# An attention-then-MLP kernel on one core: its opening re-ordered, with ungated loads, weight loads tied to landings, and mask products and casts moved between engines

## The chip, the core and the metric

The kernel runs on one core of a Trainium2 chip. The core has TensorE (PE in the profile; its weight loads are PEld), VectorE (DVE), ScalarE (ACT), GpSimd (POOL) and SyncE (SP), each with an instruction queue of its own that it works through in order, and 16 DMA engines that all queues share. The metric is the time of one execution in device microseconds (us), median of 3 runs.

## The reference

Attention with a decay per head, in blocks over the sequence, followed by a two-layer MLP with a leaky slope per hidden unit. Inputs and output are fp32; B, H, S, D = 4, 8, 768, 64; the MLP has 512 inputs and outputs and 2048 hidden units.

```python
rel = pos[:, None] - pos[None, :]
Dmask = np.where(rel >= 0, lam[:, None, None] ** rel, 0.0)
for b in range(S // block):
    qb, kb, vb = q[:, :, sl], k[:, :, sl], v[:, :, sl]      # sl: block b
    intra = (qb @ kb.T * Dmask) @ vb                         # per batch and head
    inter = (qb * lam ** (pos + 1)) @ kv_state
    out[:, :, sl] = intra + inter
    kv_state = lam ** block * kv_state + (kb * lam ** (block - 1 - pos)).T @ vb
x = out.transpose(0, 2, 1, 3).reshape(B * S, H * D)
h = x @ w_in
y = (np.maximum(h, 0) + alpha * np.minimum(h, 0)) @ w_out
```

## The kernel before, in words

**Tiling.** The 3072 tokens are cut into 6 chunks `c` of 512 tokens. A chunk is 256 positions (two blocks of 128) of two batches `bi`, and each batch is cut into two halves of four heads, `hh`. Such a quarter of a chunk is a *unit*: units 0 to 3 are chunk 0, 4 to 7 chunk 1, and so on to 23. `load(c, bi)` (line 81) loads k, q and v of one batch of a chunk, three DMAs of 512 KB issued from SP (the first, for chunk 0, in two halves of 256 KB); so `load(0, 0)` feeds units 0 and 1, `load(0, 1)` units 2 and 3. There are five raw buffers of each of k, q and v. `load_win(i)` and `load_wout(i)` (lines 95, 101) load a quarter of each weight from the POOL queue, 512 KB once they are fp16; quarter `i` of w_in serves hidden tiles `f` = 4i to 4i+3.

**A unit's attention.** `casts(n, eng)` (line 209) turns k, q, v into fp16 on the three engines that the three letters of `eng` name (V is DVE, A is ACT, G is POOL), and makes `kdec`, k times its decay, on POOL. `transposes(n)` (line 229) turns k and q on PE and copies the result to `qkT` on DVE; `decayed(n)` (line 246) makes `qdT`, q times its decay, on POOL. `cluster(old, new)` (line 260) issues on PE the products with the state (`qdT` by `RD`) and `sm` by v of unit `old`, and the scores `s` and the state update of unit `new`; DVE multiplies `s` by `dmask` into `sm` and updates the state `R`, POOL copies `R` to `RD` for the next cluster, and ACT copies the finished output of `old` to `xT`. `decay_mask(hp)` (line 167) makes the masks of a pair of heads: an exponential on ACT and a product with `keep` on POOL for each head.

**The MLP.** `up(c, f, bi)` (line 370) is four PE products for hidden tile `f` of chunk `c`, then ACT `m` (L388) and DVE `g` (L397); without `bi` it takes the whole chunk (512 columns, a *full* up), with it one batch (256 columns, a *half* up). Early ups rotate over three PSUM buffers. `down(c, t, part, 4)` (line 404) is four products of the second layer; after the fourth part ACT evacuates and issues the store.

**Order.** The order within each engine is that of the program text (`manual_schedule`), and it is written out by hand for chunks 0 and 1 (lines 466 to 541). From line 543 a rule takes over: `weave` spreads the ten attention steps of the next chunk evenly between ups of this chunk and downs of the last. The first such weave lies between lines 543 and 544 and has 16 downs of chunk 0 and units 8 to 11. Two small DMAs, `gate(0, ...)` and `gate(1, ...)` (lines 501, 536), read from w_in's third and w_out's third quarter and stand in SP's queue ahead of the loads of chunk 1 and of chunks 2 and 3, so that those are issued only when the weight quarters have landed. The transfers issued from SP and ACT (hardware_dynamic in the profile: the loads and the stores) take turns on eight DMA semaphores, and an issue waits until the transfer that had its semaphore has landed.

Of the kernel before, what the change touches and what calls it, by code (L numbers as in the profile page):

```python
# [11 lines left out]
def kernel(  # L12
# [195 lines left out]

    def casts(n, eng):
        c, bi, hh = units[n]  # L210
        kr, qr, vr = (
            t[:, ds(4 * hh, 4), :].rearrange("p h (e d) -> p e h d", e=2) for t in raws[c, bi]
        )
        t = T[n] = {}
        for name, src, e in zip(("k16", "q16", "v16"), (kr, qr, vr), eng):
            t[name] = half_pool.tile([128, 2, 4, D], fp16, tag=name, name=name)
            copy_on(e, t[name], src)
        if True:
            kdec = half_pool.tile([128, 2, 4, D], fp16, tag="kdec", name="kdec")
            for e in range(2):  # L220
                nc.gpsimd.tensor_tensor(  # L221
                    out=kdec[:, e],
                    in0=kr[:, e],
                    in1=kdecay[:, ds(4 * hh, 4), e].unsqueeze(2).to_broadcast([128, 4, D]),
                    op=ALU.mult,
                )
            t["kdec"] = kdec
# [290 lines left out]
    load_wout(1)  # L518
    for f in range(6):
        up(1, f, 0, True)  # L520
    transposes(6, "V")
    for f in range(6, 8):
        up(1, f, 0, True)
    cluster(None, 6)
# [63 lines left out]
```

## Time and profile before

| | us |
|---|---|
| median of 3 runs | 256.09 (255.88 to 256.97) |
| profiled execution | 256.11 |
| its span, first to last instruction | 254.0 |
| PE busy in the span | 215.7 (85%) |
| DVE, ACT, POOL busy | 139.3, 110.3, 116.8 |

The profiled execution is the median to within 0.02 us, and 2.1 us of it lie outside the span. PE is the busiest engine. Where a row has "[1.62 <-POOL RD L364]", the engine stood idle for 1.62 us before that instruction and the thing named ended the wait. A busy PE is not PE at its peak, since the ends of matmuls are modelled; the length of a run of equal matmuls tells its pace.

### The profile page before, as it was taken

Reading aid. Unit: us, or ns where it says so; the run is one execution under the profiler, and the core shown is the slowest. Engines: PE = TensorE matmul, PEld = TensorE weight load, DVE = VectorE, ACT = ScalarE, POOL = GpSimd, SP = SyncE. Lnnn points to the kernel's source line nnn. Section 1 sums busy time; section 2 is a strip of 40 time slices with the busy share of each in tenths; the row PEclk is TensorE's granted clock in tenths of the full one; section 3 lists DMA queues with packets and bytes.
Section 4 is the critical chain, followed back from the end, with each engine's and each line's share of the span. In section 5 each row is a group of like instructions: output and inputs, shape, how many; then the busy total and the mean of one; then the engine's idle time right before and its main releaser. Section 6 shows DMA issues by size and latency. Waiting matters only on the chain.

```text
span 254.0 us, 5553 instructions
## 1 busy us (share of the span) xinstructions
PE 215.7 (85%) x2233; PEld 119.8 (47%) x2233; DVE 139.3 (55%) x284; ACT 110.3 (43%) x210; POOL 116.8 (46%) x225
## 2 busy tenths in 40 slices
PE   0445669749687989699999999999999999999994
PEld 0323556337463554245555455554555544444453
DVE  6414767756976545147676476763676653443100
ACT  4912346525376121244544544446345453444211
POOL 3899536177604688643476437647274600000000
PEclk9999999977999999799999999999999999999999
DMA  5994997016899999999101110111011101111122
GB/s 145 291 161 69 177 305 183 3 6 105 119 228 291 290 310 301 296 320 266 45 3 43 44 41 3 41 44 41 3 41 44 41 5 41 41 41 44 41 83 83
DMA packets 45517, 29.72 MB, mean 117 GB/s; under 512 B 1316, under 2 KB 42548, under 8 KB 45492
## 3 DMA queue, kind: packets, MB, share of 16 engines
q1 hardware_dynamic: 37524, 18.89, 28.6%
q0 software_dynamic: 4224, 4.19, 11.2%
q10 hardware_dynamic: 3744, 6.30, 6.7%
q8 instruction: 17, 0.28, 0.5%
q14 instruction: 8, 0.07, 0.1%
HBM read 27.28 MB, written 6.29 MB: 132 GB/s over the span
## 4 chain that ended last, share of the span: by engine, by line
PE 68%; POOL 9%; DMA 8%; DVE 6%; ACT 4%; issue 3%; ACTq 0%; POOLq 0%; DVEq 0%
PE h_ps L380 30%; PE o_ps L410 24%; PE o_ps L433 5%; DMA kraw<-in_k_dram 3%; DMA qraw<-in_q_dram 3%; DVE g L397 2%; PE tp L235 2%; POOL qdT L250 2%; POOL dmask L171 2%; PE acc L304 2%; ACT m L388 2%; PE s L292 2%; PE acc L275 2%; DMA lam_sb<-in_lam_dram 2%; POOL RD L364 1%
## 5 line engine op out<-in xcount | busy, mean ns | idle before, releaser
L397 DVE SCALAR_TENSOR_TENSOR g<-m,oma,h_ps 128x512 f16<-128x512 f32 (+1 forms) x118 | 75.2, 647 | 73.4 <-ACT m L388 72.5
L380 PE MATMUL h_ps<-xT,w_in_sb 128*128 128x512 f16 (+1 forms) x472 | 102.1, 353 | 3.0 <-DVE g L397 1.1
L388 ACT ACTIVATE m<-h_ps 128x512 f32<-128x512 f32 (+1 forms) x118 | 61.1, 517 | 71.9 <-PE h_ps L380 69.3
L410 PE MATMUL o_ps<-w_out_sb,g 128*128 128x512 f16 x320 | 82.3, 382 | 2.6 <-DVE g L397 1.5
L380 PEld LDWEIGHTS <-w_in_sb 128*128 128x128 f16 x472 | 46.6, 102 | 41.4 <-issue 6.7
L410 PEld LDWEIGHTS <-g 128*128 128x128 f16 x320 | 30.0, 98 | 36.6 <-issue 4.4
L250 POOL TENSOR_TENSOR qdT<-qkT,qdecay 128x512 f16<-128x512 f16 x24 | 27.9, 1162 | 42.0 <-DVE qkT L205 41.7
L330 DVE TENSOR_TENSOR sm<-s,dmask 128x512 f16<-128x512 f32 x48 | 31.0, 684 | 12.3 <-POOL dmask L171 6.6
L364 POOL COPY RD<-R 64x128 f16<-64x128 f16 x80 | 23.6, 294 | 28.3 <-DVE R L351 19.5
L337 ACT ACTIVATE xT<-acc 128x512 f16<-128x512 f32 x24 | 14.3, 597 | 36.6 <-PE acc L319 18.9
L221 POOL TENSOR_TENSOR kdec<-kraw,kdecay 128x256 f16<-128x256 f32 x48 | 28.5, 613 | 0.0
L423 ACT ACTIVATE o_sb<-o_ps 128x512 f32<-128x512 f32 (+1 forms) x25 | 14.5, 580 | 25.0 <-PE o_ps L410 13.9
L275 PE MATMUL acc<-qdT,RD 128*128 128x128 f16 x80 | 9.0, 226 | 16.0 <-POOL RD L364 12.2
L205 DVE COPY qkT<-tp 128x1024 f16<-128x1024 f16 x24 | 16.5, 687 | 5.7 <-PE tp L235 5.6
L207 POOL CAST v<-vraw 128x512 f16<-128x512 f32 x24 | 14.7, 613 | 4.8 <-DMA vraw<-in_v_dram 4.7
L275 PEld LDWEIGHTS <-RD 128*128 128x128 f16 x80 | 6.0, 98 | 22.0 <-POOL RD L364 14.5
L207 POOL CAST k<-kraw 128x512 f16<-128x512 f32 x20 | 12.2, 609 | 8.0 <-DMA kraw<-in_k_dram 7.7
L351 DVE SCALAR_TENSOR_TENSOR R<-R,rdecay,acc 128x64 f16<-128x64 f16 x64 | 14.3, 275 | 2.6 <-ACT xT L337 2.2
L235 PE MATMUL tp<-ident,k 128*128 128x128 f16 x96 | 9.8, 227 | 6.4 <-DVE k L205 6.4
L203 ACT ACTIVATE q<-qraw 128x512 f16<-128x512 f32 x23 | 13.7, 621 | 3.2 <-DMA kraw<-in_k_dram 2.8
L433 PE MATMUL o_ps<-w_out_sb,g 128*128 128x512 f16 (+1 forms) x80 | 14.0, 337 | 0.0
L292 PE MATMUL s<-qkT 64*64 64x128 f16 x384 | 10.5, 229 | 2.8 <-DVE qkT L205 2.5
(46 smaller groups left out, 101.3 us busy)
## 6 DMA issues: line engine op xcount, KB each, us to landing
out_dram<-o_sb ACTq DMA_DIRECT2D x23, 256.0 KB, 2.0
kraw<-in_k_dram SPq DMA_DIRECT2D x11, 512.0 KB, 7.2
qraw<-in_q_dram SPq DMA_DIRECT2D x11, 512.0 KB, 7.6
vraw<-in_v_dram SPq DMA_DIRECT2D x11, 512.0 KB, 7.4
w_in_sb<-in_moe_w_in_dram POOLq DMA_DIRECT2D x4, 512.0 KB, 5.7
w_out_sb<-in_moe_w_out_dram POOLq DMA_DIRECT2D x4, 512.0 KB, 5.7
kraw<-in_k_dram SPq DMA_DIRECT2D x2, 256.0 KB, 5.2
qraw<-in_q_dram SPq DMA_DIRECT2D x2, 256.0 KB, 6.1
```

The source lines that it names most:

```text
L205: nc.vector.tensor_copy(out=out, in_=in_)
L207: nc.gpsimd.tensor_copy(out=out, in_=in_)
L221: nc.gpsimd.tensor_tensor(out=kdec[:, e], in0=kr[:, e], in1=kdecay[:, ds(4 * hh, 4), e].unsqueeze(2).to_broadcast([128, 4, D]), op=ALU.mult,)
L250: nc.gpsimd.tensor_tensor(out=qdT, in0=t["qkT"][:, 0], in1=qdecay[:, ds(2 * hh, 2), :].rearrange("p h (e j) -> p h e j", e=2), op=ALU.mult,)
L275: nc.tensor.matmul(ot[a][:, hp, :].rearrange("p (e j) -> p e j", e=2), lhsT=RD[bb, ho][:, a, hp].rearrange("p h d -> p (h d)"), rhs=to["qd ...
L330: nc.vector.tensor_tensor(out=sm, in0=s[hl], in1=dmask[:, hl, ds(2 * hh, 2)], op=ALU.mult)
L364: nc.gpsimd.tensor_copy(out=RD[b, hh][p, a, :, hl, :], in_=R[b, hh, 2 * pb + a][p])
L380: nc.tensor.matmul(h_ps[:, 0:n] if bi is None else h_ps[:, 0:n].rearrange("p (e j) -> p e j", e=2), lhsT=w_in_sb[:, gi, ts(f, 128)], rhs=x ...
L388: nc.scalar.activation(m[:, 0:n], h_ps[:, 0:n], AF.Relu, scale=-1.0)
L397: nc.vector.scalar_tensor_tensor(out=g, in0=mv, scalar=oma[:, f : f + 1], in1=hv, op0=ALU.mult, op1=ALU.add)
L410: nc.tensor.matmul(o_ps, lhsT=lhs(c, f, t), rhs=w_out_sb[:, f, :], start=(f == 0), stop=(f == NF - 1),)
L433: nc.tensor.matmul(o_ps[:, 0:n], lhsT=lhs(c, f, t), rhs=w_out_sb[:, f, ts(x, n)], start=(f == 0), stop=(f == NF - 1),)
```

## The change

The decay masks' product with `keep` goes from eight POOL products to four wider ones on DVE, and the exponentials of all of pair 0 and 1 now stand ahead of `kdecay`. Casts are issued tile by tile and go to other engines: k of units 2 and 3 from DVE to ACT, q of unit 1 stays on ACT and its k goes from ACT to DVE, k of units 4 and 5 from POOL to ACT. `decayed` of chunks 0 and 1 makes only the half of `qdT` that is read. SP issues `load(1, 0)`, `load(1, 1)` and `load(2, 0)` right after `load(0, 1)`, and `load(2, 1)`, `load(3, 0)`, `load(3, 1)` behind them; both gates are gone, and what holds the later three is the release of their buffers. In place of the second gate a one-element POOL copy of unit 6's k stands ahead of `load_wout(0)` on POOL's queue. The two first w_in quarters are issued together, the fourth after the casts of unit 4. The written order of chunks 0 and 1 changes: eight instead of ten tiles of chunk 0 and ten instead of twelve of chunk 1 go as two halves, the full ups of chunk 0 stand between the steps of units 4 and 5, and the last four ups of chunk 1 go into the first weave.

```diff
-    def gate(i, w):
-        nc.sync.dma_start(out=gates[:, i : i + 1], in_=w)
...
             nc.scalar.activation(dmask[:, hl, hp], rel_f, AF.Exp, scale=loglam[:, h : h + 1])
-            nc.gpsimd.tensor_tensor(out=dmask[:, hl, hp], in0=dmask[:, hl, hp], in1=keep, op=ALU.mult)
+        nc.vector.tensor_tensor(
+            out=dmask[:, :, hp], in0=dmask[:, :, hp], in1=keep.unsqueeze(1).to_broadcast([128, 2, 2, L]), op=ALU.mult
+        )
...
+    def after(n, x):
         c, bi, hh = units[n]
+        nc.gpsimd.tensor_copy(out=gates, in_=raws[c, bi]["kqv".index(x)][0:1, 4 * hh, 0:1])
...
+        p = ds(64, 64) if c < 2 else ds(0, L)
         nc.gpsimd.tensor_tensor(
-            out=qdT,
-            in0=t["qkT"][:, 0],
+            out=qdT[:, :, :, p],
+            in0=t["qkT"][:, 0, :, :, p],
...
+    for c, bi in ((1, 0), (1, 1), (2, 0)):
+        load(c, bi)
...
-    casts(2, "VAG")
+    cast(2, "k16", "A")
+    cast(2, "q16", "A")
+    cast(2, "v16", "G")
+    key_decayed(2)
     load_win(2)
-    for f in range(4):
-        up(0, f, 0, True)
-    casts(3, "VAG")
-    load_win(3)
+    run(half_ups(0, 0, range(4)))
     transposes(2, "V")
+    cast(3, "k16", "A")
+    cast(3, "q16", "A")
+    cast(3, "v16", "G")
+    key_decayed(3)
+    up(0, 4, 0, True)
     cluster(None, 2)
     transposes(3, "V")
-    for f in range(4, 8):
-        up(0, f, 0, True)
+    run(half_ups(0, 0, (5, 6)))
     cluster(2, 3)
-    for f in range(8, 10):
-        up(0, f, 0, True)
+    up(0, 7, 0, True)
     cluster(3, None)
-    for f in range(10):
-        up(0, f, 1, True)
-
-    gate(0, w_in_sb[0:1, 0, 1024:1025])
-    for bi in range(2):
-        load(1, bi)
-    for f in range(10, 14):
-        up(0, f, None, True)
-    casts(4, "GAG")
-    casts(5, "GAG")
+    casts(4, "AAG")
+    load_win(3)
+    run(half_ups(0, 1, range(8)))
+    run(ups(0, range(8, 10)))
     transposes(4, "V")
-    up(0, 14, None, True)
+    run(ups(0, range(10, 11)))
+    casts(5, "AAG")
     cluster(None, 4)
+    run(ups(0, range(11, 12)))
     transposes(5, "V")
-    up(0, 15, None, True)
+    run(ups(0, range(12, 13)))
+    after(6, "k")
+    load_wout(0)
     cluster(4, 5)
-    load_wout(0)
+    run(ups(0, range(13, 15)))
     cluster(5, None)
...
-    for f in range(12):
-        up(1, f, 1, True)
-    gate(1, w_out_sb[0:1, 8, 0:1])
-    for c in (2, 3):
-        for bi in range(2):
-            load(c, bi)
-    for f in range(12, NF):
-        up(1, f, None, True)
+    run(half_ups(1, 1, range(10)))
+    for c, bi in ((2, 1), (3, 0), (3, 1)):
+        load(c, bi)
+    run(ups(1, range(10, 12)))
...
+    for f in range(12, NF):
+        moe.insert(2 * (f - 12), lambda f=f: up(1, f))
+    weave(attention_steps(2), moe)
```

POOL's queue in the opening, before, from the last index row to the fourth `RD` copy (L171 is the mask product, L207 the cast of v, L221 `kdec`, L96 a quarter of w_in, L250 `qdT`):

```order
L154 IOTA pos_i 128x256
L171 TENSOR_TENSOR dmask<-dmask,keep 128x256 x4
L207 CAST v_224<-vraw 128x512
L221 TENSOR_TENSOR kdec<-kraw,kdecay 128x256 x2
L96 DMA w_in_sb<-in_moe_w_in_dram 128x4x512
L364 COPY RD_0_132<-R_0_1_92 64x2x64 x2
L250 TENSOR_TENSOR qdT<-qkT,qdecay 128x512
L207 CAST v_293<-vraw 128x512
L221 TENSOR_TENSOR kdec<-kraw,kdecay 128x256 x2
L96 DMA w_in_sb<-in_moe_w_in_dram 128x4x512
L171 TENSOR_TENSOR dmask<-dmask,keep 128x256 x4
L250 TENSOR_TENSOR qdT<-qkT,qdecay 128x512
```

The same place after the change (L209 is the cast of v, L228 `kdec`, L382 the copy to `RD`, L268 `qdT`):

```order
L151 IOTA pos_i 128x256
L209 CAST v_231<-vraw 128x512
L228 TENSOR_TENSOR kdec<-kraw,kdecay 128x256 x2
L382 COPY RD_0_132<-R_0_1_92 64x2x64 x2
L209 CAST v_304<-vraw 128x512
L96 DMA w_in_sb<-in_moe_w_in_dram 128x4x512 x2
L268 TENSOR_TENSOR qdT<-qkT,qdecay 128x4x64
L228 TENSOR_TENSOR kdec<-kraw,kdecay 128x256 x2
L382 COPY RD_1_133<-R_1_1_97 64x2x64 x2
L268 TENSOR_TENSOR qdT<-qkT,qdecay 128x4x64
```

Both blocks of four mask products left the queue, the first two quarters of w_in moved behind unit 0's `RD` copy and unit 1's v, and `RD` of unit 1 stands right behind its `kdec`.

SP's queue after the load of `alpha`, before, with what each issue waits for (DMAHW is one of those eight semaphores, DMASW one of a weight quarter; a name's number tells one buffer use from another):

```order
L87 DMA vraw_156<-in_v_dram 128x8x128 [waits DMAHW2_49]
L110 DMA gates_142<-w_in_sb_140 1x1 [waits DMAHW3_49,DMASW2_49]
L87 DMA kraw_753<-in_k_dram 128x8x128 [waits DMAHW4_49]
L87 DMA qraw_754<-in_q_dram 128x8x128 [waits DMAHW5_49]
L87 DMA vraw_755<-in_v_dram 128x8x128 [waits DMAHW6_49]
L87 DMA kraw_759<-in_k_dram 128x8x128 [waits DMAHW7_49]
L87 DMA qraw_760<-in_q_dram 128x8x128 [waits DMAHW0_49]
L87 DMA vraw_761<-in_v_dram 128x8x128 [waits DMAHW1_49]
L110 DMA gates_142<-w_out_sb_141 1x1 [waits DMAHW2_49,DMASW6_49]
L87 DMA kraw_1371<-in_k_dram 128x8x128 [waits DMAHW3_49]
```

The same place after the change (vraw_156 is the last of chunk 0, kraw_1322 the first of `load(2, 1)`):

```order
L87 DMA vraw_156<-in_v_dram 128x8x128 [waits DMAHW2_49]
L87 DMA kraw_209<-in_k_dram 128x8x128 [waits DMAHW3_49]
L87 DMA qraw_210<-in_q_dram 128x8x128 [waits DMAHW4_49]
L87 DMA vraw_211<-in_v_dram 128x8x128 [waits DMAHW5_49]
L87 DMA kraw_215<-in_k_dram 128x8x128 [waits DMAHW6_49]
L87 DMA qraw_216<-in_q_dram 128x8x128 [waits DMAHW7_49]
L87 DMA vraw_217<-in_v_dram 128x8x128 [waits DMAHW0_49]
L87 DMA kraw_221<-in_k_dram 128x8x128 [waits DMAHW1_49]
L87 DMA qraw_222<-in_q_dram 128x8x128 [waits DMAHW2_49]
L87 DMA vraw_223<-in_v_dram 128x8x128 [waits DMAHW3_49]
L87 DMA kraw_1322<-in_k_dram 128x8x128 [waits DMAHW4_49,DVE_49,Pool_49]
```

Nine loads stand behind chunk 0's without a wait on a weight quarter, and the tenth waits for the readers of its buffer.

## Rows read from the trace of the kernel before

**Rows 1.** The page, part 2: PE busy tenths and granted clock in 40 slices.

```profile
PE   0445669749687989699999999999999999999994
PEclk9999999977999999799999999999999999999999
```

**Rows 2.** Busy time by stretch: us, length, PE PEld DVE ACT POOL, PEclk, DMA share, GB/s.

```profile
23.59:37.15 13.56, 9.30 (x156) 7.01 (x156) 9.72 (x23) 5.91 (x14) 7.44 (x13) 1.00 1.01 206
37.15:56.55 19.40, 14.23 (x180) 8.74 (x180) 13.97 (x28) 9.66 (x21) 9.14 (x16) 0.93 0.33 76
56.55:81.43 24.88, 20.09 (x226) 13.91 (x226) 18.57 (x40) 14.45 (x34) 11.23 (x20) 0.92 0.93 177
81.43:106.77 25.34, 21.56 (x305) 11.72 (x305) 10.98 (x28) 5.62 (x10) 18.60 (x37) 0.97 1.11 299
50.44:53.85 3.41, 1.05 (x50) 0.77 (x50) 3.37 (x8) 0.94 (x2) 1.74 (x3) 1.00 0.00 0
```

**Rows 3.** Timeline of the opening: start us, us, engine, line, operation, [idle before <-releaser].

```profile
9.50 1.38 DVE L330 TENSOR_TENSOR sm<-s,dmask 128x512 f16<-128x512 f32 x2 [1.38 <-POOL dmask L171]
...
11.80 0.93 POOL L96 DMA_DIRECT2D w_in_sb<-in_moe_w_in_dram  x1
...
14.67 0.37 PE L275 MATMUL acc<-qdT,RD 128*128 128x128 f16 x2 [1.42 <-POOL qdT L250]
...
17.10 2.76 POOL L171 TENSOR_TENSOR dmask<-dmask,keep 128x256 f32<-128x256 f32 x4
19.22 1.37 DVE L330 TENSOR_TENSOR sm<-s,dmask 128x512 f16<-128x512 f32 x2 [5.24 <-POOL dmask L171]
...
21.92 0.39 PE L275 MATMUL acc<-qdT,RD 128*128 128x128 f16 x2 [4.95 <-POOL RD L364]
...
23.59 3.12 PE L380 MATMUL h_ps<-xT,w_in_sb 128*128 128x256 f16 x14 [0.16 <-ACT xT L337]
```

**Rows 4.** Groups by line, 0 to 110 us: count | busy us, mean ns | idle before.

```profile
L221 POOL TENSOR_TENSOR kdec<-kraw,kdecay 128x256 f16<-128x256 f32 x28 | 16.6, 612 | 0.0
L250 POOL TENSOR_TENSOR qdT<-qkT,qdecay 128x512 f16<-128x512 f16 x12 | 13.9, 1159 | 12.8 <-DVE qkT L205 12.5
L364 POOL COPY RD<-R 64x128 f16<-64x128 f16 x32 | 9.6, 300 | 11.6 <-DVE R L348 6.4 <-DVE R L351 4.2
L207 POOL CAST v<-vraw 128x512 f16<-128x512 f32 x14 | 8.6, 612 | 4.8 <-DMA vraw<-in_v_dram 4.7
L205 DVE COPY qkT<-tp 128x1024 f16<-128x1024 f16 x12 | 8.3, 688 | 5.7 <-PE tp L235 5.6
L203 ACT ACTIVATE q<-qraw 128x512 f16<-128x512 f32 x13 | 7.7, 621 | 3.2 <-DMA kraw<-in_k_dram 2.8 <-ACT o_sb L423 0.4
L348 DVE CAST R<-acc 128x128 f16<-128x128 f32 x8 | 2.3, 282 | 1.5 <-PE acc L319 1.5
```

**Rows 5.** The page, part 6: issues of w_in quarters, KB each, us to landing.

```profile
w_in_sb<-in_moe_w_in_dram POOLq DMA_DIRECT2D x4, 512.0 KB, 5.7
```

**Rows 6.** DMA queues 13.5 to 14.5 us: packets, MB, share of 16 engines.

```profile
q1 hardware_dynamic: 334, 0.17, 61.8%
q0 software_dynamic: 50, 0.05, 48.5%
```

**Rows 7.** The same from 14.5 to 16.5 us, when the loads of chunk 0 are in.

```profile
q0 software_dynamic: 389, 0.40, 122.7%
```

**Rows 8.** Timeline after the opening, columns as in the third group.

```profile
37.56 1.26 ACT L388 ACTIVATE m<-h_ps 128x256 f32<-128x256 f32 x3 [0.47 <-PE h_ps L380]
...
39.15 1.26 ACT L388 ACTIVATE m<-h_ps 128x256 f32<-128x256 f32 x3 [0.33 <-PE h_ps L380]
...
81.43 1.89 PE L410 MATMUL o_ps<-w_out_sb,g 128*128 128x512 f16 x8 [1.47 <-DVE g L397]
...
102.67 0.60 ACT L337 ACTIVATE xT<-acc 128x512 f16<-128x512 f32 x1 [5.01 <-DMA qraw<-in_q_dram]
...
106.77 1.87 PE L380 MATMUL h_ps<-xT,w_in_sb 128*128 128x512 f16 x4
```

More of the change, by code (lines that the diff above doesn't have):

```diff
@@ L105, in load_wout @@
         )
-    gates = const.tile([1, 4], fp16, name="gates")
-    def gate(i, w):
-        nc.sync.dma_start(out=gates[:, i : i + 1], in_=w)
+    gates = const.tile([1, 1], fp32, name="gates")
     load(0, 0, 2)
@@ L207, in copy_on, with raw_of, cast, key_decayed @@
             nc.gpsimd.tensor_copy(out=out, in_=in_)
+    def raw_of(n):
+        c, bi, hh = units[n]
+        return {
+            x + "16": t[:, ds(4 * hh, 4), :].rearrange("p h (e d) -> p e h d", e=2)
+            for x, t in zip("kqv", raws[c, bi])
+        }
+    def cast(n, name, eng):
+        t = T.setdefault(n, {})
+        t[name] = half_pool.tile([128, 2, 4, D], fp16, tag=name, name=name)
+        copy_on(eng, t[name], raw_of(n)[name])
+    def key_decayed(n):
+        hh = units[n][2]
+        kr = raw_of(n)["k16"]
+        kdec = half_pool.tile([128, 2, 4, D], fp16, tag="kdec", name="kdec")
+        for e in range(2):
+            nc.gpsimd.tensor_tensor(
+                out=kdec[:, e],
+                in0=kr[:, e],
+                in1=kdecay[:, ds(4 * hh, 4), e].unsqueeze(2).to_broadcast([128, 4, D]),
+                op=ALU.mult,
+            )
+        T[n]["kdec"] = kdec
     def casts(n, eng):
+        for name, e in zip(("k16", "q16", "v16"), eng):
+            cast(n, name, e)
+        key_decayed(n)
+    def after(n, x):
         c, bi, hh = units[n]
[L211 to L227, printed above, removed]
+        nc.gpsimd.tensor_copy(out=gates, in_=raws[c, bi]["kqv".index(x)][0:1, 4 * hh, 0:1])
     def transposes(n, eng, decay=True):
@@ L464, in weave, with half_ups, ups, run @@
                 i += 1
-    casts(0, "VVG")
+    for c, bi in ((1, 0), (1, 1), (2, 0)):
+        load(c, bi)
+    def half_ups(c, bi, fs):
+        return [lambda f=f: up(c, f, bi, True) for f in fs]
+    def ups(c, fs):
+        return [lambda f=f: up(c, f, None, True) for f in fs]
+    def run(steps):
+        for x in steps:
+            x()
+    cast(0, "k16", "V")
+    cast(0, "q16", "V")
+    cast(0, "v16", "G")
+    transposes(0, "V", False)
+    decay_mask(0)
+    decay_mask(1)
+    key_decay()
+    state_decay()
+    key_decayed(0)
+    cluster(None, 0)
+    cast(1, "k16", "V")
+    cast(1, "q16", "A")
+    cast(1, "v16", "G")
     load_win(0)
-    transposes(0, "V", False)
-    cluster(None, 0)
+    load_win(1)
     query_decay(0)
@@ L472 @@
     decayed(0)
-    casts(1, "AAG")
-    load_win(1)
     decay_mask(2)
     decay_mask(3)
+    transposes(1, "V", False)
+    key_decayed(1)
     query_decay(2)
     query_decay(3)
-    transposes(1, "V")
     cluster(0, 1)
+    decayed(1)
     slopes()
     cluster(1, None)
-    casts(2, "VAG")
+    cast(2, "k16", "A")
+    cast(2, "q16", "A")
+    cast(2, "v16", "G")
+    key_decayed(2)
     load_win(2)
-    for f in range(4):
-        up(0, f, 0, True)
-    casts(3, "VAG")
-    load_win(3)
+    run(half_ups(0, 0, range(4)))
@@ L515 @@
     cluster(5, None)
     casts(6, "GAG")
-    casts(7, "GAG")
[L518 to L524, printed above, removed]
+    load_wout(1)
+    run(ups(0, range(15, 16)))
+    run(half_ups(1, 0, range(2)))
+    transposes(6, "V")
+    run(half_ups(1, 0, range(2, 4)))
+    casts(7, "GAG")
     load_wout(2)
     load_wout(3)
+    cluster(None, 6)
+    run(half_ups(1, 0, range(4, 6)))
     transposes(7, "V")
-    for f in range(8, 10):
-        up(1, f, 0, True)
+    run(half_ups(1, 0, range(6, 8)))
@@ L530 @@
     cluster(6, 7)
-    for f in range(10, 12):
-        up(1, f, 0, True)
+    run(half_ups(1, 0, range(8, 10)))
     cluster(7, None)
-    for f in range(12):
-        up(1, f, 1, True)
-    gate(1, w_out_sb[0:1, 8, 0:1])
-    for c in (2, 3):
-        for bi in range(2):
-            load(c, bi)
+    run(half_ups(1, 1, range(10)))
+    for c, bi in ((2, 1), (3, 0), (3, 1)):
+        load(c, bi)
+    run(ups(1, range(10, 12)))
+    moe = [lambda x=x: down(0, x // 4, x % 4, 4) for x in range(16)]
@@ L540 @@
     for f in range(12, NF):
-        up(1, f, None, True)
-    weave(attention_steps(2), [lambda x=x: down(0, x // 4, x % 4, 4) for x in range(16)])
+        moe.insert(2 * (f - 12), lambda f=f: up(1, f))
+    weave(attention_steps(2), moe)
     for c in range(2, NC):
```

12 lines of the change are left out of this document (6 added, 6 removed).

## The prediction

> **What bounds the kernel now.** I read the page's slices first. From about 108 us on PE is busy in every slice and at its full clock, so the end is set by when PE gets there; what the change can win lies before [rows 1]. The stretches tell how much: PE is idle for 4.3 of 13.56 us (23.59 to 37.15), for 5.2 of 19.40, 4.8 of 24.88 and 3.8 of 25.34 us [rows 2]. I call these stages B, C, D and E: B ends with the xT of unit 3, C with that of unit 5, D with the first down, E with the first up of chunk 2. Stage A is what lies before 23.59.
>
> The timeline of A shows its chain: unit 1's sm waits 5.24 us for the second block of mask products on POOL, PE then waits 4.95 us for RD, and only behind that do the first ups run without a gap [rows 3]. Those ups take 3.12 us for 14 products of 256 columns, 223 ns each, while three halves of four products each later go by in 1.59 us [rows 3, 8]. [...] Late in E ACT stands for 5.01 us until a load of q lands, though it next does an xT that reads no q [rows 8]: what holds it is the store ahead of it, whose semaphore is that load's.
>
> **Stage A.** On DVE two mask products come in ahead of unit 0's sm. The trace has no such product on DVE. Its bounds are 0.35, half of the copy to qkT with twice the elements, and 1.38, the two POOL products of 0.69 that each replaces [rows 3, 4]. I take sm's 0.69, which has the same width and fp32 inputs. From the end of the first qkT at 8.1 they fill the 1.38 us that sm waited [rows 3], so sm ends at 10.9 as before. POOL then does R's copy (0.28 on DVE, 2 x 0.30 on POOL) until 11.8, v of unit 1 (0.61), two w_in issues (0.93 for the first) and half a qdT (half of 1.16) until 14.8 [rows 3, 4]. PE waited for qdT until 14.67 before: nothing is won up to there. Behind it the wait goes: sm of unit 1 starts when its scores are there, about 15.7 instead of 19.22, and all that follows is 3.5 us earlier, the ups at 20.1 instead of 23.59.
>
> But the ups need w_in. A quarter lands 5.7 us after its issue [rows 5], of which 512 KB at 0.40 MB in 2.0 us are 2.6 us [rows 7], so 3.1 are fixed. Now the ungated loads run beside it. In the one microsecond of the trace where both queues are busy the weights have 48.5 and the loads 61.8% of the engines [rows 6]: 44%, or 88 KB/us, 5.8 us for a quarter. Issued at 12.4, the first lands at 21.3 and the second at 27.1. With equal turns (100 KB/us) these are 20.6 and 25.7; with the bytes of that microsecond, half of which is start-up (50 KB/us), 25.7 and 36. I take 88. The ups start at 21.3: A wins **2.3**.
>
> [...]
>
> **Stage B.** Four halves at 223 ns a product take 3.6 us, to 24.9. The next up, tile 4, needs the second quarter and stands on PE ahead of unit 2's scores, so PE and the attention both wait until 27.1. From there the chain runs through DVE: the up with m and g takes a buffer's round, 1.59 us [rows 8]; unit 2's sm 1.38; R three times 0.28; qkT 0.69; two g at the m's pace of 0.42; unit 3's sm 1.38; R 0.28; RD 0.60; then PE about 0.6 and xT about as long as a cast, 0.62 [rows 3, 4, 8]. That ends at 35.9. Moving two casts of k from DVE to ACT takes two copies out of this chain; on ACT they stand between m's, where it has time. B lasts 14.6 us instead of 13.56 and holds two halves less: it **loses 1.0**. The later quarters are needed at 40 and 47; the third lands at 33, the fourth, issued behind unit 4's kdec at about 37, near 46.
>
> **Stage C.** Before, PE was busy for 14.23 us [rows 2], some 1.6 of them at the low clock after 53.85, so 13.4 at the full one. Two halves less (0.53 each) and one full up more (0.87; eight products take 1.89 with their tail [rows 8]) make 13.2. PE waits remain: ACT casts k and q of unit 4 (1.24) ahead of the first m, and the spare PSUM buffers cover 0.3 of it (0.9); unit 4's qkT stands on DVE behind the g of tile 9 (0.75); RD of unit 4 (0.35), unit 5's qkT behind sm, R and a g (1.0), RD of unit 5 (0.55). That is 3.5 and makes 16.7. What goes are the two waits of some 2 us for RD, because full ups now stand between the steps.
>
> To this I add the clock. Around 29 to 34 PE has little to do in the new order, 1.4 us of work in 4.6, much as in the stretch of 1.05 in 3.41 before which the clock was high and after which it was low [rows 1, 2]. If four of the eight halves then run at 4 x 223 ns instead of 530, that is 1.5 us. C: 18.2, wins **1.2**. [...]
>
> **Stage D.** Busy 20.09, 4.1 of it at the low clock up to 60.7, so 18.0. Four halves less (2.1) and a net of one full up less (tiles 12 to 15 go to E, tile 15 of chunk 0 and tiles 10 and 11 come) leave 15.0. The waits of units 6 and 7 are built as before (sm, R, two g and qkT in a row on DVE): 4.8 before [rows 2], less a net 0.6, as the 1.47 us go in which the first down waited for g [rows 8] and as fewer halves stand between the steps. 4.2 and 15.0 are 19.2: D wins **5.7**.
>
> **Stage E.** Busy 21.56, less 0.9 for the low clock from 105.05; four full ups more are 3.5: 24.2. Of the 3.8 idle some 2.4 are the wait behind the store. Its semaphore is now one of the loads of `load(3, 1)` or `load(4, 1)`, which can be issued when units 5 and 9 have been cast and not when w_out has landed, so 1.4 stay: 25.6. It **loses 0.3**, and the up after 106.77, which took 1.87 us for four products [rows 8], **wins 0.9**.
>
> Sum: 2.3 - 1.0 + 1.2 + 5.7 - 0.3 + 0.9 = 8.8. What follows is the same work on a busy PE. The profiled execution took 256.1, its median is the same: **247.3 us**.
>
> **Rivals.** *The clean case:* the queues take equal turns (second quarter at 25.7, 1.4 us) and the clock stays high (1.5 us): 244.4. For it: shares of 44 to 50% are close, and from 27 to 50 us, with waits of 1 to 2 us on PE, the clock stayed high before [rows 1].
>
> *The late wait stays:* the loads of chunks 2 and 3 come behind w_out's quarters, the stores' semaphores again wait for loads, and E keeps its 2.4 us, its 0.9 and the 0.9 behind it: 251.5. Against it: after stage B the loads have 30 us more than before; for it: three of them still stand in SP's order behind buffers.
>
> *The change doesn't do what it says, the masks cost DVE what they cost POOL:* 1.38 instead of 0.69 each, four of them on DVE's chain of units 0 and 1, 2.8 us. The attention is then ready at 22.9 and not at 20.1, the ups come 1.6 later than at 21.3: 249.0. Against: DVE is the faster one in every operation that both do in these rows.
>
> *Slower: the weights starve.* If the loads keep the weights at 50 KB/us or below, a quarter of what they have alone, the fourth quarter lands at 56 and not at 46, the ups from tile 12 on stand still, and the 8.8 us are gone; at 45 KB/us it lands at 60.5, 13 us late: 260. For it: the bytes of the one shared microsecond; against it: the share of engine time there.
>
> **How the numbers follow.** Forecast 0.50, clean 0.20, late wait 0.12, dear masks 0.08, starved 0.10. The range runs from below the clean case to the late wait: 243.5 to 251.5; it leaves out the starved case and the edges of two others. About 0.5% (1.3 us) is what a measurement of this kernel can tell from no change. Of the starved case 0.08 is slower by more than that and 0.02 within it, as is 0.02 of late wait and masks together: faster 0.88, same 0.04, slower 0.08.
>
> **What would show it.** Stage A: mask rows of about 0.7 on DVE, no wait of sm for a mask, ups at about 21. Stage B: PE idle before tile 4's up with a release by w_in; if it isn't, the share was better. Clock: a low stretch around 34 to 38. C and D: no RD wait near 2 us, no low clock at 54 to 60. E: no store that holds ACT for 2 us or more. The prediction is wrong if the weights' landings move by more than 4 us from 21, 27, 33 and 46, or if PE is idle for over 5 us in D or E.

## The result, and the profile after

The changed kernel takes **245.5 us**, median of 4 runs (244.65 to 246.12); the kernel before, on the same chip, takes 256.04. The ratio is 0.958 with an interval of 0.954 to 0.962. The forecast was 247.3, its range 243.5 to 251.5: the time lies inside, 1.8 us under the forecast and 1.1 over the *clean* rival.

The profiled execution took 244.65, its span 242.8. A second one, of a later measurement of the same kernel (a_again below), took 245.68 and is nearer to the median. The slices of the first, PE busy in tenths and the granted clock, answer [rows 1]:

```profile
PE   0345758886999889999999999999999999999993
PEclk9999999998899999999999999999999999999999
```

PE's row holds 8 and 9 from the eleventh slice on; before it does so from the eighteenth. The two low clocks of before at 54 to 61 and at 105 us (granted 0.50 in both) are gone; one at 59 to 62, 0.50 too, is left. By stage, as in [rows 2] (us, length, then PE, PEld, DVE, ACT and POOL busy, granted clock, DMA share, GB/s), this is the changed kernel, B to E and the low-clock stretch:

```profile
21.67:34.10 12.43, 8.95 (x150) 6.26 (x151) 8.51 (x20) 5.11 (x13) 5.41 (x12) 1.00 1.17 262
34.10:50.31 16.21, 13.78 (x178) 8.22 (x178) 13.39 (x27) 10.19 (x23) 7.51 (x16) 1.00 1.08 276
50.31:70.95 20.64, 17.22 (x210) 12.07 (x209) 15.22 (x35) 11.42 (x27) 12.62 (x23) 0.92 1.15 244
70.95:96.34 25.39, 23.27 (x317) 12.62 (x316) 14.32 (x33) 8.64 (x15) 14.98 (x31) 1.00 0.64 180
58.97:62.38 3.41, 3.41 (x67) 2.41 (x70) 2.47 (x6) 1.33 (x3) 1.48 (x4) 0.50 1.19 253
```

and this the second execution, C and D:

```profile
34.44:51.75 17.31, 15.28 (x178) 8.88 (x178) 13.47 (x27) 10.31 (x22) 7.52 (x16) 0.90 1.12 275
51.75:71.97 20.22, 15.82 (x210) 11.19 (x209) 15.01 (x35) 11.35 (x28) 12.67 (x23) 1.00 1.18 254
```

| stage | predicted | first execution | second |
|---|---|---|---|
| A, to the first ups | 21.3 | 21.67 | 22.07 |
| B, to the xT of unit 3 | 14.6 | 12.43 | 12.37 |
| C, to the xT of unit 5 | 18.2 | 16.21 | 17.31 |
| D, to the first down | 19.2 | 20.64 | 20.22 |
| E, to the first up of chunk 2 | 25.6 | 25.39 | 25.39 |
| the rest of the span | 146.3 | 146.5 | 146.5 |
| outside the span | 2.1 | 1.8 | 1.8 |

The opening, as in [rows 3] (L168 is the mask product, L348 `sm`, L398 an up's product):

```profile
8.02 1.28 DVE L168 TENSOR_TENSOR dmask<-dmask,keep 128x512 f32<-128x512 f32 x2
...
15.94 1.29 DVE L348 TENSOR_TENSOR sm<-s,dmask 128x512 f16<-128x512 f32 x2 [1.16 <-PE s L310]
...
21.67 3.45 PE L398 MATMUL h_ps<-xT,w_in_sb 128*128 128x256 f16 x16 [1.71 <-DMA w_in_sb<-in_moe_w_in_dram]
25.85 0.61 PE L398 MATMUL h_ps<-xT,w_in_sb 128*128 128x256 f16 x4 [0.29 <-DMA w_in_sb<-in_moe_w_in_dram]
```

The first pair of masks takes 1.28 us on DVE, 0.64 each, where two POOL products took 1.38 for one; the second pair takes 2.17 (see the last section). Unit 1's `sm` waits for its scores and no longer 5.24 us for a mask. The first ups wait for w_in (1.71), and tile 4 waits for the second quarter, but only 0.29.

A quarter of w_in lands 9.0 us after its issue (median of four), where [rows 5] had 5.7. First the row of the page's part 6, then the DMA queues from 19 to 23 us, in the middle of these transfers (packets, MB, share of 16 engines):

```profile
w_in_sb<-in_moe_w_in_dram POOLq DMA_DIRECT2D x4, 512.0 KB, 9.0
```

```profile
q0 software_dynamic: 566, 0.56, 82.7%
q1 hardware_dynamic: 566, 0.29, 35.0%
```

The four landed at 21.62, 25.80, 29.53 and 42.69 us.

### The profile page after: what moved, and what is told of

It is laid out like the page before. It is cut to its first block, busy times and chain, and to the rows that moved or that the text cites. A ratio compares the mean times of both kernels' runs of the same rounds, so it can differ in the third digit from the quotient of the medians.

```text
span 242.8 us, 5500 instructions
## 1 busy us (share of the span) xinstructions
PE 212.2 (87%) x2217; PEld 117.1 (48%) x2217; DVE 140.6 (58%) x283; ACT 110.5 (45%) x209; POOL 106.2 (44%) x216
## 4 chain that ended last, share of the span: by engine, by line
PE 76%; DVE 7%; DMA 6%; ACT 5%; POOL 3%; issue 3%; POOLq 0%; ACTq 0%
PE h_ps L398 30%; PE o_ps L428 29%; PE o_ps L451 6%; DMA w_in_sb<-in_moe_w_in_dram 4%; DVE g L415 3%; PE tp L252 3%; PE s L310 3%; PE acc L322 2%; PE acc L293 2%; DMA lam_sb<-in_lam_dram 2%; DVE sm L348 1%; DVE qkT L207 1%; ACT m L406 1%; POOL RD L382 1%; ACT o_sb L441 1%
## 5 line engine op out<-in xcount | busy, mean ns | idle before, releaser
L415 DVE SCALAR_TENSOR_TENSOR g<-m,oma,h_ps 128x512 f16<-128x512 f32 (+1 forms) x114 | 74.4, 662 | 71.6 <-ACT m L406 71.1
L398 PE MATMUL h_ps<-xT,w_in_sb 128*128 128x512 f16 (+1 forms) x456 | 100.3, 353 | 4.6 <-DMA w_in_sb<-in_moe_w_in_dram 2.0
L406 ACT ACTIVATE m<-h_ps 128x512 f32<-128x512 f32 (+1 forms) x114 | 59.9, 529 | 71.3 <-PE h_ps L398 69.9
L398 PEld LDWEIGHTS <-w_in_sb 128*128 128x128 f16 x456 | 43.8, 100 | 42.4 <-issue 4.2
L268 POOL TENSOR_TENSOR qdT<-qkT,qdecay 128x512 f16<-128x512 f16 (+1 forms) x24 | 23.9, 998 | 53.8 <-DVE qkT L207 53.5
L348 DVE TENSOR_TENSOR sm<-s,dmask 128x512 f16<-128x512 f32 x48 | 30.8, 683 | 8.8 <-PE s L310 8.5
L382 POOL COPY RD<-R 64x128 f16<-64x128 f16 x80 | 23.1, 288 | 27.4 <-DVE R L369 19.0
L228 POOL TENSOR_TENSOR kdec<-kraw,kdecay 128x256 f16<-128x256 f32 x48 | 28.8, 620 | 1.0 <-ACT kdecay L176 1.0
L441 ACT ACTIVATE o_sb<-o_ps 128x512 f32<-128x512 f32 (+1 forms) x25 | 14.5, 580 | 23.4 <-PE o_ps L428 12.4
L207 DVE COPY qkT<-tp 128x1024 f16<-128x1024 f16 x24 | 16.4, 685 | 2.0 <-PE tp L252 2.0
L209 POOL CAST v<-vraw 128x512 f16<-128x512 f32 x24 | 14.7, 612 | 4.3 <-DMA vraw<-in_v_dram 4.2
L252 PEld LDWEIGHTS <-k 128*128 128x128 f16 x96 | 7.3, 100 | 12.3 <-DVE k L207 7.8
```

Of the source, the lines that this page charges most:

```text
L207: nc.vector.tensor_copy(out=out, in_=in_)
L228: nc.gpsimd.tensor_tensor(out=kdec[:, e], in0=kr[:, e], in1=kdecay[:, ds(4 * hh, 4), e].unsqueeze(2).to_broadcast([128, 4, D]), op=ALU.mult,)
L252: nc.tensor.transpose(tp[:, x, hp, e, :], t[name][:, e, ds(2 * hp, 2), :].rearrange("p h d -> p (h d)"), ident,)
L268: nc.gpsimd.tensor_tensor(out=qdT[:, :, :, p], in0=t["qkT"][:, 0, :, :, p], in1=qdecay[:, ds(2 * hh, 2), :].rearrange("p h (e j) -> p h e ...
L348: nc.vector.tensor_tensor(out=sm, in0=s[hl], in1=dmask[:, hl, ds(2 * hh, 2)], op=ALU.mult)
L382: nc.gpsimd.tensor_copy(out=RD[b, hh][p, a, :, hl, :], in_=R[b, hh, 2 * pb + a][p])
```

## The experiments

Each time is a median, each ratio is to the kernel before on the same chip, with its 95% interval. Names that begin with a_ are the changed kernel with the edit shown, those with b_ the kernel before with it.

### The masks

**a_mask_pool**: the products go back to POOL.

```diff
-        nc.vector.tensor_tensor(
-            out=dmask[:, :, hp], in0=dmask[:, :, hp], in1=keep.unsqueeze(1).to_broadcast([128, 2, 2, L]), op=ALU.mult
-        )
+            nc.gpsimd.tensor_tensor(out=dmask[:, hl, hp], in0=dmask[:, hl, hp], in1=keep, op=ALU.mult)
```

> The changed kernel with one part undone: the mask products are eight POOL products again, each behind its exponential. Theory (the parts add up, the masks are the opening's part): POOL has 2 x 2.8 us more ahead of unit 0's kdec and of unit 1's RD, unit 1's sm waits for a mask again, the first ups come at about 24 instead of 21.7 us, and about 2.5 us arrive at the end: 248.0. Rival (the gain comes from the ungated loads alone): the opening is 2 to 3 us later but later stages wait for data anyway, 245.5 to 246.

248.01 us, 0.969 [0.965, 0.973]: 2.5 more than the changed kernel. Its timeline shows the old wait again:

```profile
16.13 2.76 POOL L168 TENSOR_TENSOR dmask<-dmask,keep 128x256 f32<-128x256 f32 x4
...
18.25 1.37 DVE L346 TENSOR_TENSOR sm<-s,dmask 128x512 f16<-128x512 f32 x2 [3.05 <-POOL dmask L168]
...
23.82 0.61 PE L396 MATMUL h_ps<-xT,w_in_sb 128*128 128x256 f16 x2
```

The ups start at 23.82 instead of 21.67, and the 2.15 us are still there at the end.

**b_mask_dve**: the same move alone, in the kernel before (the diff reversed).

> The kernel before with one part of the change alone: mask products on DVE, one for two heads, nothing else moved. Theory: w_in's first quarter landed at 17.7 us there and is not what the ups wait for, so they start at about 20.3 instead of 23.6, and 2 to 3.3 us arrive at the end: 253.0 to 254.0. Rival (loads alone): the late wait of the first weave eats it, 255.5 to 256.

256.32 us, 1.002 [0.998, 1.006]: no difference. The theory fell, and its rival was right on the number; the trace shows two causes, the rival's and one that no theory had. The first is on DVE:

```profile
7.72 0.69 DVE L171 TENSOR_TENSOR dmask<-dmask,keep 128x512 f32<-128x512 f32 x1 [2.50 <-ACT dmask L170]
8.90 1.11 DVE L171 TENSOR_TENSOR dmask<-dmask,keep 128x512 f32<-128x512 f32 x1 [0.49 <-ACT dmask L170]
...
10.52 0.43 DVE L207 CAST k<-kraw 128x512 f16<-128x512 f32 x1
```

The mask's place in the text of before is ahead of unit 0's casts. On POOL that cost the casts nothing; on DVE the product waits 2.50 us for ACT's exponentials with the cast of k queued behind it, and k is cast at 10.52 instead of 5.87. The ups start at 22.99 (22.82 before, by the same row), the first down comes at 80.72 instead of 81.43. The second cause takes those 0.7 us too: stage E grows from 25.34 to 26.68. This execution took 257.64, 1.3 above its median, and its clock is lower, 0.971 over the span where before has 0.980. In E its four products by `RD` at 104.61 take 0.61 us, and those of before at 104.31, ahead of the low stretch from 105.05, 0.50: PE is slow earlier, and that adds to E behind the rows shown. ACT there:

```profile
96.36 0.60 ACT L425 ACTIVATE o_sb<-o_ps 128x512 f32<-128x512 f32 x1 [1.00 <-PE o_ps L412]
102.58 0.35 ACTq L428 DMA_DIRECT2D out_dram<-o_sb  x1
102.98 0.60 ACT L339 ACTIVATE xT<-acc 128x512 f16<-128x512 f32 x1 [6.03 <-DMA qraw<-in_q_dram]
```

The output tile is ready at 96.96, its store is issued at 102.58, and xT stands behind it. This is [rows 8]'s wait of 5.01, now 6.03: its end follows a load's landing and not what PE has done, for `xT` comes at 102.98 where it came at 102.67, although the downs began 0.7 earlier.

**b_ungated_mask**: the gates gone and the mask products behind unit 0's transposes, where the changed kernel has them.

```diff
-    decay_mask(0)
     kdecay = const.tile([128, H, 2], fp32, name="kdecay")
...
-    decay_mask(1)
...
     transposes(0, "V", False)
+    decay_mask(0)
+    decay_mask(1)
     cluster(None, 0)
```

> The kernel before without its gates (loads issued as in the changed one) and with the mask products on DVE behind unit 0's casts and transposes, where the changed kernel has them; all else as before. Theory: the masks on DVE alone gained nothing since they stood ahead of unit 0's cast of k on DVE's queue and held it for 4.65 us; placed behind it, the ups start near 20.2 instead of 22.82, nothing later holds them back without the gates, and of the 252.2 us without gates 2.6 go: 249.6. Rival: in the old order of products the earlier start is given back behind the opening, by one more low-clock stretch in stage C or by the waits of units 4 and 5, as the first down of the changed kernel in the old order (80.81 us) suggests, which comes only 0.2 us before that of the kernel without gates: 251.5 to 252.2.

249.5 us, 0.979 [0.974, 0.983], 2.7 less than without the gates alone (next): the theory's 249.6. The ups start at 19.55, the earliest of all kernels here. The first w_in quarter, issued at 9.27, has landed at 18.0, so the attention alone sets their start:

```profile
18.66 0.39 PE L274 MATMUL acc<-qdT,RD 128*128 128x128 f16 x2 [2.02 <-POOL RD L363]
18.98 0.64 PE L303 MATMUL acc<-sm,v 64*64 64x128 f16 x16
19.55 0.61 PE L379 MATMUL h_ps<-xT,w_in_sb 128*128 128x256 f16 x2
```

The place of the masks on DVE's queue decides the opening, and without the gates the gain lasts: the first down comes at 77.36, against 81.01 in b_ungated. What this place is worth with the gates was not run.

### The gates

**b_ungated**: the kernel before with its loads issued as in the changed one.

```diff
+    for c, bi in ((1, 0), (1, 1), (2, 0)):
+        load(c, bi)
     casts(0, "VVG")
...
-    gate(0, w_in_sb[0:1, 0, 1024:1025])
-    for bi in range(2):
-        load(1, bi)
...
-    gate(1, w_out_sb[0:1, 8, 0:1])
-    for c in (2, 3):
-        for bi in range(2):
-            load(c, bi)
+    for c, bi in ((2, 1), (3, 0), (3, 1)):
+        load(c, bi)
```

> The kernel before with both gates gone and the loads issued where the changed kernel has them in SP's order; nothing else moved. Theory: only the first weave gains, its 2.4 us behind a store and the low clock at 105 us (1.7): 252.0. Rival (loads alone): most of the gain, 246 to 248. A third outcome, the loads slow the weights: slower than 256.

252.2 us, 0.986 [0.981, 0.991], as expected. Up to the first down it runs like before (81.01 against 81.43); stage E is 22.21 instead of 25.34, and the low clock at 105 is gone: the four products of an up take 1.03 us at 104.95, where those of before took 1.87 at 106.77.

**a_gated**: both gates put back into the changed kernel.

```diff
-    for c, bi in ((1, 0), (1, 1), (2, 0)):
-        load(c, bi)
...
     load_win(2)
+    gate(0, w_in_sb[0:1, 0, 1024:1025])
+    for bi in range(2):
+        load(1, bi)
...
-    for c, bi in ((2, 1), (3, 0), (3, 1)):
+    gate(1, w_out_sb[0:1, 8, 0:1])
+    for c, bi in ((2, 0), (2, 1), (3, 0), (3, 1)):
```

> The changed kernel with both gates of the kernel before back: loads of chunk 1 behind w_in's third quarter, loads of chunks 2 and 3 behind w_out's third. Theory: w_in lands without company (first quarter near 18, ups at 20.1 us, 1.6 us won), the loads of chunks 2 to 4 come 15 to 20 us later and the stores' semaphores again wait for them (ACT held for some us at 80 to 90), 3 to 6 us lost there: 247 to 250. Rival (loads alone): all of the gain goes, 254 to 256.

245.51 us, 0.962 [0.957, 0.967]: no difference. Both theories fell. The stretches of its profiled execution, the longest of four (247.48), point to why, B to E:

```profile
20.01:33.21 13.20, 9.92 (x154) 6.83 (x151) 8.51 (x20) 6.61 (x16) 5.67 (x12) 0.92 0.73 154
33.21:50.97 17.76, 15.94 (x178) 9.43 (x178) 13.64 (x27) 10.41 (x23) 8.79 (x18) 0.86 0.68 136
50.97:71.18 20.21, 15.82 (x210) 11.18 (x209) 15.01 (x35) 11.33 (x27) 8.69 (x16) 1.00 0.99 187
71.18:98.86 27.68, 23.29 (x318) 12.61 (x317) 14.41 (x33) 8.65 (x15) 19.03 (x38) 1.00 1.12 297
```

With the loads held back, w_in lands at 18.25 and 20.78, and the ups start at 20.01 instead of 21.67: 1.7 us are won. Stage E is 2.3 longer, and on ACT the store waits as before:

```profile
84.67 0.60 ACT L445 ACTIVATE o_sb<-o_ps 128x512 f32<-128x512 f32 x1 [1.98 <-PE o_ps L432]
89.35 0.34 ACTq L448 DMA_DIRECT2D out_dram<-o_sb  x1
```

In the changed kernel the same store is issued at 85.06, right behind its tile. So what the held loads gain in the opening, the later loads about lose in stage E; which share of that is the second gate's alone was not run. Part of B and C in this execution is a low clock: the rows have 0.92 and 0.86, and at 0.50 that is 7 us, some 31 to 38, against 3.5 by the 0.90 in C of the second execution. In the old order the first gained nothing: the ups of b_ungated start at 22.83, those of before at 22.82, both behind the attention and not behind w_in.

**a_gate_q2**: a gate on the second quarter of w_in alone, none later, and the w_out move of a_wout_late (next part).

```diff
-    for c, bi in ((1, 0), (1, 1), (2, 0)):
-        load(c, bi)
...
     load_win(2)
+    gate(0, w_in_sb[0:1, 0, 512:513])
+    for c, bi in ((1, 0), (1, 1), (2, 0)):
+        load(c, bi)
     run(half_ups(0, 0, range(4)))
...
-    load_wout(2)
-    load_wout(3)
     cluster(None, 6)
...
     cluster(6, 7)
+    load_wout(2)
+    load_wout(3)
```

> The changed kernel with w_out's last two quarters behind unit 6's RD copies, and the loads of chunk 1 and of (2, 0) held back by a one-element DMA until w_in's second quarter has landed; no gate behind that. Theory: w_in's first two quarters then move alone, as they do in the kernel with both gates, whose ups started at 20.01 us instead of 21.67 and whose tile 4 did not wait; what that kernel gave back came from its later gate (its stage E was 2.3 us longer) and from loads that started only at 26. With loads from 21 us on, ups at 20.0, the xT of unit 3 by 33.3, stages C to E as in the kernel with w_in early and w_out late (16.6, 19.1, 25.4): 242.6 us. Rival: the time between opening and first down is the clock's and not the loads': an earlier opening moves the low stretch to where PE has more to do (31 to 38 us, stage C 17.8), and the time stays at 243.6 to 244.5.

**242.53 us**, 0.951 [0.946, 0.956], the theory's 242.6 and the lowest time here, though its interval overlaps that of a_both (next part). Of the 3.0 us to the changed kernel some 1.2 are the w_out move, as a_wout_late measures it alone. The stages are 19.92, 13.35, 16.78, 19.05 and 25.39. PE, at the ups and at tile 4:

```profile
19.92 0.61 PE L402 MATMUL h_ps<-xT,w_in_sb 128*128 128x256 f16 x2
...
24.48 1.06 PE L402 MATMUL h_ps<-xT,w_in_sb 128*128 128x256 f16 x4
```

Neither waits for w_in.

### The weights

The next four ran on one chip, where the kernel before took 256.23.

**a_again**, the changed kernel as it is:

> The changed kernel once more, on the chip of the next three, so that differences under 1% can be read: 245.5 by every theory, with one or two low-clock stretches of TensorE in the span.

245.46 us, 0.964 [0.957, 0.970].

**a_win0_early**: w_in's first quarter issued behind unit 0's v.

```diff
     cast(0, "v16", "G")
+    load_win(0)
...
-    load_win(0)
     load_win(1)
```

> The changed kernel with w_in's first quarter issued by POOL right behind unit 0's v, where POOL waits about 1 us for kdecay, instead of behind unit 1's v. Theory (attention is ready at 20.0 us and the ups wait 1.7 us for that quarter alone): ups at about 20.1, no wait before tile 4, about 1.5 us less: 244.0. Rival (the loads of unit 2 and 3 come later for it, or the chain of DVE sets the pace of the stretch to 34 us): 245.5.

244.7 us, 0.961 [0.956, 0.967]: half of what was expected, and not told apart from a_again by its interval. The quarter, issued at 7.70, lands at 16.02, and the ups don't wait for it; but they start at 21.00 and not at 20. The timeline shows where the time goes:

```profile
12.02 3.69 DVE L168 TENSOR_TENSOR dmask<-dmask,keep 128x512 f32<-128x512 f32 x2
15.63 0.68 DVE L207 COPY qkT<-tp 128x1024 f16<-128x1024 f16 x1
...
13.33 0.69 POOL L268 TENSOR_TENSOR qdT<-qkT,qdecay 128x256 f16<-128x256 f16 x1
13.97 1.18 POOL L228 TENSOR_TENSOR kdec<-kraw,kdecay 128x256 f16<-128x256 f32 x2
...
16.37 0.64 PE L310 MATMUL s<-qkT 64*64 64x128 f16 x16 [1.92 <-DVE qkT L207]
```

With one issue less ahead of them, `qdT` and `kdec` of unit 1 now run on POOL beside the second pair of masks, and that pair takes 3.69 us on DVE; in the changed kernel it starts at 12.02 as well and takes 2.17, beside the cast of v and the two issues. All exponentials are done by 11.92 in both. So the scores start 1.1 us later (15.26 there), and the attention gives back what the weights won.

**a_wout_late**: w_out's last two quarters behind unit 6's `RD` copies.

```diff
-    load_wout(2)
-    load_wout(3)
     cluster(None, 6)
...
     cluster(6, 7)
+    load_wout(2)
+    load_wout(3)
     run(half_ups(1, 0, range(8, 10)))
```

> The changed kernel with w_out's third and fourth quarter issued behind unit 6's RD copies instead of ahead of them. Theory (PE waits 1.5 us for that RD at 58.7 because POOL issues two quarters first, and the low clock from 59.0 follows from the empty stretch): RD at about 56.6, no low clock near 59, 2 to 3 us less: 243.0. Rival (the PE stretch is set by DVE, or the quarters then come too late for the third and fourth down): 245.5 or more.

244.23 us, 0.958 [0.953, 0.963], again about half. POOL and PE of the changed kernel (L102 is the issue of w_out, L382 the copy to `RD`), and behind it of this one:

```profile
56.45 1.54 POOL L102 DMA_DIRECT2D w_out_sb<-in_moe_w_out_dram  x2
57.98 0.65 POOL L382 COPY RD<-R 64x128 f16<-64x128 f16 x2
...
58.69 0.28 PE L293 MATMUL acc<-qdT,RD 128*128 128x128 f16 x2 [1.49 <-POOL RD L382]
```

```profile
57.96 0.63 POOL L382 COPY RD<-R 64x128 f16<-64x128 f16 x2
...
58.65 0.29 PE L293 MATMUL acc<-qdT,RD 128*128 128x128 f16 x2
...
61.99 0.29 PE L293 MATMUL acc<-qdT,RD 128*128 128x128 f16 x2 [1.14 <-POOL RD L382]
```

The 1.49 go, and D takes 19.07 instead of 20.22 (a_again):

```profile
51.81:70.88 19.07, 15.83 (x211) 11.18 (x209) 14.93 (x35) 11.34 (x27) 12.60 (x23) 1.00 1.17 249
```

The other half of the expected gain was a low clock at 59, and that did not follow from the wait: a_again, on the same chip, has the same wait (1.50) and no low clock there (1.00 over D).

**a_both**: the two together.

> Both of the last two edits. Theory (two separate waits): the sum, 241.5. Rival (the second hides the first): as the better of the two.

243.56 us, 0.957 [0.952, 0.962]: the two add up (0.8 and 1.2 against 1.9 us). The forecast of 241.5 was 2.1 too low since it added the two gains as expected and not as they came.

### The order and the casts

**a_old_order**: the changed opening with the old order of products from unit 2 on, the old places of casts and weight issues among them, and the first weave without ups (cut to the main lines).

```diff
-    up(0, 4, 0, True)
     cluster(None, 2)
...
-    run(half_ups(0, 1, range(8)))
-    run(ups(0, range(8, 10)))
+    run(half_ups(0, 1, range(10)))
+    run(ups(0, range(10, 14)))
...
-    run(half_ups(1, 1, range(10)))
+    run(half_ups(1, 1, range(12)))
```

> The changed kernel with the order of the kernel before for the ups and attention steps of units 2 to 7, for casts and weight issues among them, and the first weave without ups; masks, casts' engines, loads without gates and the opening stay changed. Theory (the order is what fills PE between 37 and 60 us): two waits of about 2 us for RD and a low clock near 54 to 60 are back, 4 to 5 us lost: 250.0. Rival (the order is incidental, loads and opening make the gain): 245.5 to 246.5.

250.75 us, 0.979 [0.975, 0.984], near the theory's 250.0. B to E:

```profile
21.58:35.22 13.64, 9.99 (x158) 7.55 (x159) 9.38 (x22) 6.01 (x15) 6.08 (x13) 1.00 1.18 245
35.22:56.41 21.19, 15.95 (x180) 9.56 (x180) 14.13 (x28) 10.68 (x23) 7.15 (x15) 0.83 1.13 283
56.41:80.81 24.40, 19.64 (x226) 13.71 (x226) 18.52 (x40) 14.43 (x34) 12.27 (x23) 0.93 0.88 187
80.81:103.01 22.20, 20.75 (x305) 11.53 (x304) 10.88 (x28) 5.65 (x10) 14.98 (x31) 1.00 0.50 136
```

Against the second execution of the changed kernel B is 1.3 longer, C and D are 3.9 and 4.2 longer: PE idles for 5.24 us in C (21.19 less 15.95) and not for 2.03, and its clock is 0.83 there and not 0.90. E is 3.2 shorter, as the four ups of the weave are not in it. Products, casts and weight issues moved together here; which of them counts most is not shown.

**a_k_dve**: k of units 2 and 3 cast on DVE again.

```diff
-    cast(2, "k16", "A")
+    cast(2, "k16", "V")
...
-    cast(3, "k16", "A")
+    cast(3, "k16", "V")
```

> The changed kernel with the k casts of units 2 and 3 back on DVE. Theory (two copies of 0.42 us more on DVE's chain from 26 to 34 us): 0.4 to 0.8 us more, 246.1. Rival (they fit into waits of DVE, or ACT is the one that is short there): no difference, or less by up to 0.6.

245.43 us, 0.959 [0.956, 0.963]: no difference that the times can tell. One cast falls into the wait for w_in, when DVE has nothing to do. The other stands on DVE's chain; DVE here, and behind it the last row in the changed kernel:

```profile
26.78 0.42 DVE L207 CAST k<-kraw 128x512 f16<-128x512 f32 x1
...
27.77 0.68 DVE L348 TENSOR_TENSOR sm<-s,dmask 128x512 f16<-128x512 f32 x1
```

```profile
27.31 1.28 DVE L348 TENSOR_TENSOR sm<-s,dmask 128x512 f16<-128x512 f32 x2
```

So unit 2's `sm` comes 0.46 later, of the size that the theory gave it, and the xT of unit 3 is about 0.5 later; in the median that is not to be told from nothing.

## Why the prediction was right, and where it was off

**The gain has three parts, and they were the ones named.** From before to the changed kernel the runs step down: 255.8 with the gates, 252.2 without, 249.5 with the masks on DVE behind the casts, 245.5 with the new order and the rest. The steps were measured beside before on different chips, so they hold to about 1 us. The last step has two signs: a_old_order, with all but the new order, takes 250.75, so the order gains some 5 us, and the rest of the change, whose w_in comes later than that of b_ungated_mask (ups at 21.58 and 19.55), costs about 1. The total is nearer than its parts: in the two executions B and C together came in 3.1 to 4.2 us under the forecast, A and D 1.8 over, so that part of the near hit is luck.

**Stage A was right.** `sm` of unit 1 at 15.94 (15.7 predicted), ups at 21.67 (21.3), a mask of the first pair 0.64 (0.69): the rows of `sm` were a good stand-in for an operation that the trace did not have. That w_in pays for the loads was the term that made A 2.3 and not 3.5, and A won 1.9; a_gated and a_gate_q2, where the loads wait, have their ups at 20.0, the time that the prediction gave to the attention alone.

**Stage B was mis-sized by 2.2 us; the step that failed is the share of 44%.** B was to lose 1.0 and won 1.1. The first quarter's landing was met by two errors that cancel, so that stage A owes its time to luck in part: beside the loads its first bytes come at 16.35, 3.8 us after the issue (1.6 in before), and then it moves faster than 88 KB/us. From 19 to 23 us both queues send 566 packets, and the weights' are of 1 KB, the loads' of 512 bytes: 0.56 against 0.29 MB, 140 and 72 KB/us. In this window the two are equal by packets, and neither by time (82.7 and 35.0%) nor by bytes. The microsecond of [rows 6] held the start-up of the one queue and the end of the other and could not show this. So the second quarter lands at 25.80, 1.3 us before the forecast and where the clean rival had it (25.7); 0.5 more is the chain behind it (8.3 instead of 8.8), and 0.4 the later start.

**Stage C: the waits were too large, the clock term was right in size but not there in each execution.** In the second execution PE's clock goes low between 35 and 39 us (0.90 over C), and C's busy time is 15.28 (14.7 predicted with that term), its idle 2.03 instead of 3.5. In the first the clock stays high there (1.00 over C, 13.78 busy, 2.43 idle) and falls at 59 (0.50), behind the 1.49 us for RD. Between the two, C's busy time differs by 1.50, the term of the prediction; both hold 0.6 more than was put down without it. Of the ten profiled executions of the changed kernel and its variants eight have a low stretch that begins between 31 and 36 us: C's clock is 0.83 to 0.94 in a_again, a_gated, a_gate_q2, a_mask_pool and a_old_order, and the first 38 products of C take 6.6 to 7.2 us in a_wout_late, a_both and a_k_dve, against 5.6 in the changed kernel's first execution and a_win0_early, which have none there. The five waits listed for C were added up as if each came in full; in the first execution those for `RD` were 0.4 together and not 0.9, those for `qkT` 1.3 and not 1.75, that for the spare buffers 0.6 and not 0.9. Eight of ten agree with the drop in a thin stretch, and the other two show that the thin stretch alone did not decide it here. The prediction's terms for a low clock count PE at half its pace where they come off the busy times of before (C, D and E), and at 223 ns a product for 133 in the 1.5 us of C. No run shows TensorE's clock rates, nor that the 223 ns are a low clock's; the changed kernel shows eight products of 256 columns in 1.89 us at a granted 0.50 (at 60.11) and in 1.04 at 1.00 (at 27.64). The first ups run near the slow pace, 16 products in 3.45 us, with a recorded 1.00; why is not shown.

**Stage D was 1.0 to 1.4 too short.** The prediction counted RD waits built as before, and missed that two issues of w_out, 1.54 us of POOL, now stand right ahead of unit 6's `RD` copy; a_wout_late takes them out (19.07; 19.2 was predicted). That the two numbers meet is luck: D's busy time is 15.8 there, 0.8 more than the 15.0 put down, and its idle time 3.2, a microsecond less than the 4.2. In the first execution the low clock of 59 to 62 adds to it.

**Stage E came out (25.39 for 25.6) for another reason.** The prediction left 1.4 us behind a store. No store waits: in ACT's timeline each is issued 0.62 us after its tile's start. PE's 2.1 idle us are three waits of 0.7 for the evacuation `o_sb`; and the busy time is 0.9 less than put down. ACT, and PE at one of the waits:

```profile
84.44 0.60 ACT L441 ACTIVATE o_sb<-o_ps 128x512 f32<-128x512 f32 x1 [1.98 <-PE o_ps L428]
85.06 0.34 ACTq L444 DMA_DIRECT2D out_dram<-o_sb  x1
```

```profile
85.09 1.02 PE L428 MATMUL o_ps<-w_out_sb,g 128*128 128x512 f16 x4 [0.69 <-ACT o_sb L441]
```

**The rivals.** *Clean* had the second quarter's landing right, though its equal turns of 100 KB/us were not what the queues did, and the clock half. *Late wait* fell: its mechanism is there in b_mask_dve and a_gated, and the changed kernel doesn't have it. *Dear masks* fell with 0.64 and, in the second pair, 1.09 a mask: 3.45 us for the four, where 2.8 were put down and the rival had 5.5. *Starved* fell: the fourth quarter landed at 42.69, before the 46 predicted.

## What to carry to other kernels

Moving an operation to an engine that is faster at it (a mask took 0.64 us on DVE, its two products on POOL 1.38) also moves it into that engine's queue: look at what stands behind it there, and how long its own inputs keep it waiting (2.50 us in b_mask_dve). A saving ahead of a wait that a transfer ends can be worth nothing until that transfer is earlier too, so find the last such wait first. When loads are freed, hold them only until the weights that the first products need have landed: that gate brought the ups from 21.7 to 19.9 us here, while the two old gates together gave the gain back.
